# Low parts of the expert weights made on VectorE, and the last quarter of w_in converted one stage later

## The chip, the cores and the metric

One core of a Trainium2 chip runs the whole program once. The time is device microseconds of that core, one launch, median of the runs shown. Besides TensorE (PE, with its weight loads PEld) the core has VectorE (DVE), ScalarE (ACT), GpSimd (POOL) and SyncE (SP), each working through its own instruction queue in order. SP's queue issues nearly all DMAs.

## The reference

Three parts follow one another: an attention over 4 x 8 heads of 576 rows, a routed layer in which each of the 2304 rows goes to one of 8 experts, and a dense layer over all rows. The change touches the weights of the second and third parts:

```
for e in range(E):                                    # x: 2304 x 512
    h = np.maximum(x[mask] @ w1[e], 0.0)              # w1[e]: 512 x 1024
    out[mask] = gate_w[mask, None] * (h @ w2[e])      # w2[e]: 1024 x 512
h = x @ w_in                                          # w_in: 512 x 2048, given as float64
g = np.maximum(h, 0.0) + alpha * np.minimum(h, 0.0)
return (g @ w_out).astype(np.float32)                 # w_out: 2048 x 512, given as float64
```

## The kernel before

**Stages.** Attention and routing come first, with five small tiles of the busiest expert's rows computed beside them. Then come the **expert slots**: seven slots (`NSU`) of 256 rows of one expert each, run by `slot(s)` in `moe`. Then the **dense layer** in `moe2`: five blocks of rows, four of 512 and one of 256.

**Precision.** The slots and the dense layer multiply in a 32-bit matmul format that keeps only part of a float32. So every operand is split into a high part (a cast by ScalarE, L541) and a low part (operand minus high part, L542, on an engine that the caller names), and each product is three matmuls: high by high, low by high, high by low. `split` does this.

**One slot.** The raw weights of the slot's expert lie in the tile `wraw`. `split1` makes `w1h` and `w1l` for one of 8 column tiles f, low part on VectorE, in a ring of 3. `split2` makes `w2h` and `w2l` for one of 8 pieces, numbered c = 0 to 3 and u = 0, 1 (`w2l_21` is c = 2, u = 1), in a ring of 5; in the kernel before c = 0, 1 have their low parts made on GpSimd and c = 2, 3 on VectorE (L637). For each f, 12 matmuls (L700) give `h`, ScalarE takes the high part `hh` and VectorE the low part `hl` (L703). Then 24 matmuls (L720) for each c give `y`, which VectorE or ScalarE copies out (L722, L723). A slot has 192 matmuls. The rows of a later slot are loaded into `L` (`L<-xs`, L566), scaled by GpSimd (L573), transposed by VectorE (`T`, L575) and split into `xh` and `xl`; this is asked for one or two slots ahead.

**Input weights of the dense layer.** While the slots run, `W2in(i)` converts w_in, piece by piece (128 x 256, 32 pieces). A piece comes as 64-bit words by an SP load of 256 KB into one of three buffers (`raw64`), two pieces ahead. `from64` makes a float32 of it with three bit operations on VectorE (L549, L550, L551, tile `xwi`), and then splits it into `wih` and `wil`. Low parts go to GpSimd. Two pieces are done ahead of the slots (`AT0`), then six in each slot, so slots 0 to 4 do the 30 that are left.

**Dense layer.** In a block, for each of 16 column tiles f, 12 matmuls (L776) give `oh`, VectorE applies the activation (`m`, L778, L779) and makes `gl`, ScalarE makes `gh`. Four column tiles later the second product `oy` (L767) uses them. In block 0, `W2out(f)` converts row tile f of w_out in two pieces by the same `from64` and the same three buffers, low parts on GpSimd.

**Order.** The order within each engine's queue is not the source's: a scheduler places instructions by priorities and its own estimate of when each can start. After that each queue is fixed and runs in order; an instruction that waits holds back all behind it on its engine.

Of the kernel before, what the change touches and what calls it, by code (L numbers as in the profile page):

```python
# [538 lines left out]
def split(nc, hi, lo, x, lo_engine):  # L539

    nc.scalar.copy(hi,x)  # L541
    return lo_engine.tensor_tensor(out=lo,in0=x,in1=hi.bitcast(F32),op=ALU.subtract)  # L542
# [68 lines left out]
def moe(tc, stack, router, wts, rows, ep, fp, W2in):  # L611
# [22 lines left out]
        return hi,lo  # L634
    def split2(s,c,u):
        hi=kp.tile([128,4,128],F32R,tag="h2",name=f"w2h{s}_{c}{u}",bufs=5); lo=kp.tile([128,4,128],F32R,tag="l2",name=f"w2l{s}_{c}{u}",bufs=5)
        split(nc,hi,lo,wts.r2[:,4*u:4*u+4,128*c:128*c+128],nc.vector if c>1 else nc.gpsimd)  # L637
        return hi,lo
    W1={}; W2={}; after=[None]
    def whole(s, e):  # L640
# [37 lines left out]
    def slot(s):  # L678
        last=s+1==NSU
        if s==0: load_x(1); after[0]=rows.loaded  # L680
        if not last:
            e=router.reg(0,s+1,[ENG.SP],E-1); ch=router.reg(3,s+1,[ENG.SP],1)
        xh,xl=xin.pop(s)
        H=[]
        def one(s,f):
            if f<8 and (s,f) not in W1: W1[s,f]=split1(s,f)
        def two(i):
            if i<8:
                c,u=divmod(i,2); W2[i]=split2(s,c,u)
                if u and not last: wts.load2(c,e,ch)  # L690
        one(s,0); one(s,1)
        for f in range(8):
            one(s,f+2)
            if f%2 and not last: wts.load1(f//2,e,ch)
            wh,wl=W1.pop((s,f))
            h=hp.tile([128,SL],F32,tag="h",name=f"h{s}_{f}")
            n=0
            for c in range(4):
                for a,b in ((wh,xh),(wh,xl),(wl,xh)):
                    nc.tensor.matmul(h,lhsT=a[:,c],rhs=b[:,c],start=n==0,stop=n==11); n+=1  # L700
            hh=wk.tile([128,SL],F32R,tag=f"hh{f}",name=f"hh{s}_{f}",bufs=1); hl=wk.tile([128,SL],F32R,tag=f"hl{f}",name=f"hl{s}_{f}",bufs=1)
            nc.scalar.activation(out=hh,in_=h,func=AF.Relu)  # L702
            d=nc.vector.scalar_tensor_tensor(out=hl,in0=h,scalar=0.0,in1=hh.bitcast(F32),op0=ALU.max,op1=ALU.subtract)  # L703
            H.append((hh,hl))
            if 2<=f<7: two(f-2)
            if f<6:
                with tc.issue_after(d.ins), tc.issue_after(after[0].ins): W2in(AT0+6*s+f)
            if f==4 and not last: prep_x(s+1)
            if f==5 and s+2<NSU: load_x(s+2)
        o=ep.tile([128,4,SL],F32,tag="eh",name=f"yo{s}",bufs=1)  # L710
        for c in range(4):
            if c and s+1<NSU: one(s+1,c-1)
            y=yp.tile([128,SL],F32,tag="y",name=f"y{s}_{c}")
            n=0
            for u in range(2):
                wh,wl=W2[2*c+u]
                for f in range(4):
                    hh,hl=H[4*u+f]
                    for a,b in ((wh,hh),(wl,hh),(wh,hl)):
                        nc.tensor.matmul(y,lhsT=a[:,f],rhs=b,start=n==0,stop=n==23); n+=1  # L720
                two(2*c+u+5)
            if c%2: nc.vector.tensor_copy(o[:,c],y)  # L722
            else: nc.scalar.copy(o[:,c],y)  # L723
        yr=router.reg(2,s,[ENG.SP],N)
        rows.store(o,yr,SL)
# [18 lines left out]
    ti=wk.tile([128,4],U32,tag="ti",name=f"ti{j}",bufs=1)  # L744
    return load,(hi,lo,ti)

def moe2(tc, stack, wp, fp, ep, win, first, W2out, al, ysT, ytok, out):
    nc=tc.nc
    op=stack.enter_context(tc.tile_pool(name="o_const",bufs=1))
    wk=stack.enter_context(tc.tile_pool(name="o_work",bufs=2))  # L750
# [9 lines left out]
    def block(j):  # L760
# [7 lines left out]
        G=[]; LAG=4 if not last else 1  # L768
        if last: zh=wk.tile([128,16,128],F32R,tag="xh",name="zh",bufs=1); zl=wk.tile([128,16,128],F32R,tag="xl",name="zl",bufs=1)
        for f in range(16):  # L770
            if j==0: W2out(f,woh,wol)
            h=hp.tile([128,512],F32,tag="h",name=f"oh{j}_{f}")
            k=0; fs=slice(128*f,128*f+128)
            for c in range(4):
# [27 lines left out]
def body(tc,q,k,v,mod,wg,bias,w1,w2,w_in,w_out,alpha,out):  # L802
    nc=tc.nc
    with ExitStack() as ctx:
# [37 lines left out]
        def w_out_rows(f,u):  # L842
            r=staged[f,u]=wst.tile([128,256,2],I32,tag="raw64",name=f"wo{f}{u}")
            nc.sync.dma_start(r.rearrange("p d w -> p (d w)"),w_out[128*f:128*f+128,256*u:256*u+256].bitcast(I32))
        def W2out(f,woh,wol):
            for u in range(2):
                if (f,u) not in staged: w_out_rows(f,u)
                c=slice(256*u,256*u+256)
                from64(nc,wst,f"wo{f}{u}",woh[:,f,c],wol[:,f,c],staged.pop((f,u)),nc.gpsimd)
# [1 line left out]
        with nc.allow_non_contiguous_dma("alpha"):  # L851
            nc.sync.dma_start(al,alpha.rearrange("(f p) -> p f",p=128))
        with ExitStack() as s1:
            def W2in_load(i):
                c,p=divmod(i,8); c=3-c
                if c<0: return
                r=staged["in",i]=wst.tile([128,256,2],I32,tag="raw64",name=f"wi{c}{p}")
                return nc.sync.dma_start(r.rearrange("p d w -> p (d w)"),w_in[128*c:128*c+128,256*p:256*p+256].bitcast(I32))
            def W2in(i):
                W2in_load(i+2)  # L860
                c,p=divmod(i,8); c=3-c; ps=slice(256*p,256*p+256)
                if c>=0: from64(nc,wst,f"wi{c}{p}",wir[:,c,ps],wil[:,c,ps],staged.pop(("in",i)),nc.gpsimd)
            W2in_load(0); router.marks[ENG.SP]=W2in_load(1)
            router.marks[ENG.Activation]=running[2]; router.marks[ENG.Pool]=running[1]
            rare=router.flag((ENG.Pool,ENG.Activation,ENG.PE,ENG.DVE,ENG.SP))
# [12 lines left out]
            for u in range(2): w_out_rows(0,u)  # L878
        ee.close()
        with ExitStack() as s2:  # L880
            moe2(tc,s2,wp,fp,ep,(wir,wil),first,W2out,al,ysT,ytok,out)


_INS = ["q", "k", "v", "moe_modality_id", "moe_w_gate", "moe_modality_bias", "moe_w1", "moe_w2", "moe2_w_in", "moe2_w_out", "moe2_alpha"]
# [23 lines left out]
```

## Time and profile before

| | |
|---|---|
| runs | 869.8, 878.67, 886.12 us; median 878.67 |
| profiled execution | 876.93 us, of which the span is 875.2 |
| PE busy | 817.5 us (93%) |
| DVE busy | 529.2 us (60%) |
| ACT busy | 359.9 us (41%) |
| POOL busy | 263.3 us (30%) |
| first matmul of slot 0 | 282.4 us |
| last matmul of slot 6 | 469.2 us |
| end of block 0 of the dense layer | 557.15 us |

"Busy" is the time that instructions of an engine occupied. An average over the span hides that the stages have different limits, so the stages are read apart. A start time and a length are given for each instruction; VectorE takes up the next one a little before the write of the last is acknowledged, so that lengths of neighbours overlap, and the distance from start to start is what one costs in a full queue.

### The profile page before, as it was taken

How to read it: one execution, taken by the hardware profiler on the slowest of the kernel's cores; microseconds unless marked ns; L12 is line 12 of the kernel's file. 1: busy time of each engine (PE TensorE's matmuls, PEld its weight loads, DVE VectorE, ACT ScalarE, POOL GpSimd, SP SyncE). 2: the span in 40 equal slices, each digit the busy share in tenths (PEclk: the TensorE clock that was granted, in tenths of full speed). 3: DMA queues.
4: the chain of work that ended last, by engine and by line, in shares of the span. 5: the costliest groups of instructions: out<-in, count | busy, mean ns of one | idle time of the engine just before them, and what ended most of it. 6: DMA issues, size and time to landing. Idle time of an engine off the chain costs nothing.

```text
span 875.2 us, 16800 instructions
## 1 busy us (share of the span) xinstructions
PE 817.5 (93%) x6175; PEld 698.9 (80%) x6175; DVE 529.2 (60%) x1304; ACT 359.9 (41%) x863; POOL 263.3 (30%) x450
## 2 busy tenths in 40 slices
PE   5797898999997897989999999999999999999997
PEld 3465687778897887989998888888888888888895
DVE  6856756656443997999946998443344333533361
ACT  7697795885423554646542333211121111111120
POOL 9425555366331554535421432100010001000100
PEclk9877889899998998999999999999999999999999
DMA  7735676322332434539501442200020001000100
GB/s 190 172 97 161 187 200 145 101 57 55 78 91 61 98 92 79 135 114 237 157 26 61 132 147 83 85 1 0 1 91 1 0 1 55 13 0 1 37 13 25
DMA packets 96609, 71.74 MB, mean 82 GB/s; under 512 B 40456, under 2 KB 83976, under 8 KB 96520
## 3 DMA queue, kind: packets, MB, share of 16 engines
q1 hardware_dynamic: 93544, 61.02, 26.6%
q0 software_dynamic: 2976, 9.59, 3.2%
q8 instruction: 50, 0.82, 0.4%
q14 instruction: 39, 0.32, 0.1%
HBM read 76.43 MB, written 18.90 MB: 109 GB/s over the span
## 4 chain that ended last, share of the span: by engine, by line
PE 56%; DVE 3%; DMA 2%; issue 2%; ACT 0%; SPq 0%; POOL 0%; POOLq 0%; DVEq 0%; ACTq 0%
PE oh L776 23%; PE oy L767 22%; PE h L700 6%; PE y L720 5%; DMA L<-xs 1%; DVE w1l L542 1%; DVE xwi L551 1%; DVE xwi L550 0%; DMA ytok<-L 0%; DVE hl L703 0%; DVE xwi L549 0%; DMA out<-o,ti 0%; DVE T L575 0%; POOL L L573 0%; DVE xl L542 0%
## 5 line engine op out<-in xcount | busy, mean ns | idle before, releaser
L541 ACT CAST gh<-m 128x512 fp32r<-128x512 f32 (+1 forms) x80 | 44.5, 556 | 241.3 <-DVE m L779 241.3
L776 PE MATMUL oh<-oxh,wil 128*128 128x512 f32 (+1 forms) x320 | 118.9, 372 | 0.0
L776 PE MATMUL oh<-oxh,wih 128*128 128x512 f32 (+1 forms) x320 | 118.9, 371 | 0.0
L776 PE MATMUL oh<-oxl,wih 128*128 128x512 f32 (+1 forms) x320 | 118.6, 371 | 0.0
L778 DVE TENSOR_SCALAR m<-oh,al 128x512 f32<-128x512 f32 (+1 forms) x80 | 55.5, 694 | 91.4 <-PE oh L776 91.4
L793 POOL DMA_INDIRECT out<-o,ti x18 | 17.6, 980 | 308.3 <-ACT o L792 270.6
L767 PE MATMUL oy<-woh,gh 128*128 128x512 f32 x272 | 107.1, 394 | 0.0
L767 PE MATMUL oy<-wol,gh 128*128 128x512 f32 x272 | 106.7, 392 | 0.0
L767 PE MATMUL oy<-woh,gl 128*128 128x512 f32 x272 | 106.5, 393 | 0.0
L700 PE MATMUL h<-xh,w1h 128*128 128x256 f32 x224 | 67.2, 300 | 11.4 <-DVE hl L703 6.3
L542 DVE TENSOR_TENSOR gl<-m,gh 128x512 fp32r<-128x512 f32 (+1 forms) x80 | 48.9, 612 | 40.0 <-ACT gh L541 40.0
L776 PEld LDWEIGHTS oh<-oxh,wil 128*128 128x128 f32 x320 | 60.2, 188 | 11.8
L776 PEld LDWEIGHTS oh<-oxh,wih 128*128 128x128 f32 x320 | 60.1, 188 | 11.5
L776 PEld LDWEIGHTS oh<-oxl,wih 128*128 128x128 f32 x320 | 60.1, 188 | 11.3
L720 PE MATMUL y<-hh,w2h 128*128 128x256 f32 x224 | 61.9, 287 | 4.7 <-ACT hh L702 2.9
L700 PE MATMUL h<-xl,w1h 128*128 128x256 f32 x224 | 65.9, 294 | 0.0
L700 PE MATMUL h<-xh,w1l 128*128 128x256 f32 x224 | 65.6, 293 | 0.0
L720 PE MATMUL y<-hh,w2l 128*128 128x256 f32 x224 | 60.7, 286 | 2.5 <-POOL w2l L542 1.5
L767 PEld LDWEIGHTS oy<-woh,gl 128*128 128x128 f32 x272 | 51.1, 188 | 12.1
L767 PEld LDWEIGHTS oy<-wol,gh 128*128 128x128 f32 x272 | 51.0, 188 | 11.4
L767 PEld LDWEIGHTS oy<-woh,gh 128*128 128x128 f32 x272 | 51.1, 188 | 11.0
L720 PE MATMUL y<-hl,w2h 128*128 128x256 f32 x224 | 59.6, 285 | 0.1
(303 smaller groups left out, 1873.2 us busy)
## 6 DMA issues: line engine op xcount, KB each, us to landing
wraw<-in_moe_w SPq DMA_DIRECT2D x56, 512.0 KB
wi<-in_moe_w_in SPq DMA_DIRECT2D x32, 256.0 KB
wo<-in_moe_w_out SPq DMA_DIRECT2D x32, 256.0 KB
vw<-in_v SPq DMA_DIRECT2D x88, 64.0 KB
xs<-z SPq DMA_DIRECT2D x8, 528.0 KB
ldq<-in_q SPq DMA_DIRECT2D x16, 256.0 KB
ldk<-in_k SPq DMA_DIRECT2D x16, 256.0 KB
ldv<-in_v SPq DMA_DIRECT2D x8, 512.0 KB
```

What stands on the lines that cost most here:

```text
L541: nc.scalar.copy(hi,x)
L542: return lo_engine.tensor_tensor(out=lo,in0=x,in1=hi.bitcast(F32),op=ALU.subtract)
L551: nc.vector.scalar_tensor_tensor(out=xi,in0=hw,scalar=-(1<<30),in1=xi,op0=ALU.bitwise_and,op1=ALU.bitwise_or)
L700: nc.tensor.matmul(h,lhsT=a[:,c],rhs=b[:,c],start=n==0,stop=n==11); n+=1
L720: nc.tensor.matmul(y,lhsT=a[:,f],rhs=b,start=n==0,stop=n==23); n+=1
L767: nc.tensor.matmul(y[t],lhsT=a[:,ts],rhs=b[:,f],start=f==0 and k==0,stop=f==15 and k==2)
L776: nc.tensor.matmul(h[:,:n],lhsT=a[:,c,fs],rhs=b[:,c,:n],start=k==0,stop=k==11); k+=1
L778: nc.vector.tensor_scalar(out=m[:,:n],in0=h[:,:n],scalar1=0.0,scalar2=al[:,f:f+1],op0=ALU.min,op1=ALU.mult)
L793: nc.gpsimd.indirect_dma_start(out=out[:],out_offset=bass.IndirectOffsetOnAxis(ap=ti[:,t:t+1],axis=0),in_=o[:],in_offset=None,bounds_check ...
```

## The change

Low parts of `w2` are made on VectorE for all c. Of w_in, the pieces are put in another order: first columns 0 to 1535 of all four row tiles (24 pieces), then the last quarter, columns 1536 to 2047 (8 pieces). Slots 0 to 4 do four pieces each and slot 5 does two, with the low parts on VectorE as well. The last 8 pieces are converted in block 0 of the dense layer, one in each of column tiles 0 to 7, loaded through the same three buffers, one piece ahead. Low parts of w_out stay on GpSimd.

```diff
     def split2(s,c,u):
...
-        split(nc,hi,lo,wts.r2[:,4*u:4*u+4,128*c:128*c+128],nc.vector if c>1 else nc.gpsimd)
+        split(nc,hi,lo,wts.r2[:,4*u:4*u+4,128*c:128*c+128],nc.vector)
...
-            if f<6:
-                with tc.issue_after(d.ins), tc.issue_after(after[0].ins): W2in(AT0+6*s+f)
+            if f<4 and 4*s+f<22:
+                with tc.issue_after(d.ins), tc.issue_after(after[0].ins): W2in(AT0+4*s+f)
...
-            if j==0: W2out(f,woh,wol)
+            if j==0:
+                W2out(f,woh,wol)
+                if f<8: W2in(f)
...
+        PIECES=[(c,p) for c in (3,2,1,0) for p in range(6)]+[(c,p) for p in range(6,8) for c in range(4)]
+        def W2in_load(i):
+            if i>=len(PIECES): return
+            c,p=PIECES[i]
+            r=staged["in",i]=wst.tile([128,256,2],I32,tag="raw64",name=f"wi{c}{p}")
+            return nc.sync.dma_start(r.rearrange("p d w -> p (d w)"),w_in[128*c:128*c+128,256*p:256*p+256].bitcast(I32))
+        def W2in(i, ahead=2):
+            for j in range(i+1,i+ahead+1):
+                if ("in",j) not in staged and j not in done: W2in_load(j)
+            c,p=PIECES[i]; ps=slice(256*p,256*p+256); done.add(i)
+            from64(nc,wst,f"wi{c}{p}",wir[:,c,ps],wil[:,c,ps],staged.pop(("in",i)),nc.vector)
+        done=set()
...
-            def W2in(i):
-                W2in_load(i+2)
-                c,p=divmod(i,8); c=3-c; ps=slice(256*p,256*p+256)
-                if c>=0: from64(nc,wst,f"wi{c}{p}",wir[:,c,ps],wil[:,c,ps],staged.pop(("in",i)),nc.gpsimd)
...
-            moe2(tc,s2,wp,fp,ep,(wir,wil),first,W2out,al,ysT,ytok,out)
+            moe2(tc,s2,wp,fp,ep,(wir,wil),first,W2out,lambda f: W2in(24+f,1),al,ysT,ytok,out)
```

**VectorE, start of slot 0.** Before:

```order
L542 TENSOR_TENSOR w1l_0_10059<-wraw,w1h_0_10058 128x512
L542 TENSOR_TENSOR w1l_1_10063<-wraw,w1h_1_10062 128x512
L542 TENSOR_TENSOR w1l_2_10067<-wraw,w1h_2_10066 128x512
L542 TENSOR_TENSOR w2l_20_10305<-wraw,w2h_20_10304 128x512
L542 TENSOR_TENSOR w1l_3_10096<-wraw,w1h_3_10095 128x512
L703 SCALAR_TENSOR_TENSOR hl_0_10084<-h_0_10070,hh_0_10083 128x256
L549 TENSOR_SCALAR xwi_10089<-wi_4469 128x256
L550 SCALAR_TENSOR_TENSOR xwi_10089<-wi_4469,xwi_10089 128x256
L542 TENSOR_TENSOR w1l_4_10126<-wraw,w1h_4_10125 128x512
```

The same place with the change:

```order
L542 TENSOR_TENSOR w1l_2_10067<-wraw,w1h_2_10066 128x512
L542 TENSOR_TENSOR w2l_00_10147<-wraw,w2h_00_10146 128x512
L542 TENSOR_TENSOR w2l_01_10181<-wraw,w2h_01_10180 128x512
L542 TENSOR_TENSOR w2l_10_10215<-wraw,w2h_10_10214 128x512
L542 TENSOR_TENSOR w2l_11_10248<-wraw,w2h_11_10247 128x512
L542 TENSOR_TENSOR w2l_20_10289<-wraw,w2h_20_10288 128x512
L542 TENSOR_TENSOR w1l_3_10096<-wraw,w1h_3_10095 128x512
L703 SCALAR_TENSOR_TENSOR hl_0_10084<-h_0_10070,hh_0_10083 128x256
L549 TENSOR_SCALAR xwi_10089<-wi_4469 128x256
L542 TENSOR_TENSOR w1l_4_10126<-wraw,w1h_4_10125 128x512
```

Four low parts of w2 that stood in GpSimd's queue now stand on VectorE ahead of `w1l_3` and `hl_0`. GpSimd's queue holds only the scaling of `L`, once a slot, and one small cast until the slots are over.

**SP's queue, ahead of the load of slot 3's rows.** Before (`xs<-z` clears rows under a condition; then the row load `L_10675`):

```order
L561 DMA xs<-z 1024x1x132
L536 DMA wraw<-in_moe_w 128x8x128
L858 DMA wi_10514<-in_moe_w_in 128x512
L858 DMA wi_10547<-in_moe_w_in 128x512
L858 DMA wi_10582<-in_moe_w_in 128x512
L566 DMA L_10675<-xs 32x8x132
```

With the change (the row load is `L_10643`):

```order
L561 DMA xs<-z 1024x1x132
L536 DMA wraw<-in_moe_w 128x8x128
L854 DMA wi_10498<-in_moe_w_in 128x512
L854 DMA wi_10531<-in_moe_w_in 128x512
L566 DMA L_10643<-xs 32x8x132
```

Two loads of w_in instead of three stand ahead of the row load. The last one ahead waits for a buffer that VectorE frees: before by the operation right behind `hl_4` of slot 1, now by the one right behind `hl_3` of slot 1.

**VectorE, column tile 6 of block 0.** Before:

```order
L778 TENSOR_SCALAR m_6_12983<-oh_6_12970,al 128x512
L551 SCALAR_TENSOR_TENSOR xwo_12956<-wo_12954,xwo_12956 128x256
L779 SCALAR_TENSOR_TENSOR m_6_12983<-oh_6_12970,m_6_12983 128x512
L549 TENSOR_SCALAR xwo_12964<-wo_12962 128x256
L550 SCALAR_TENSOR_TENSOR xwo_12964<-wo_12962,xwo_12964 128x256
L549 TENSOR_SCALAR xwo_13004<-wo_13002 128x256
L551 SCALAR_TENSOR_TENSOR xwo_12964<-wo_12962,xwo_12964 128x256
L542 TENSOR_TENSOR gl_6_12987<-m_6_12983,gh_6_12986 128x512
```

With the change (`xwi_12802` is a piece of w_in; the lines of `moe2` have moved by two):

```order
L780 TENSOR_SCALAR m_6_12977<-oh_6_12964,al 128x512
L542 TENSOR_TENSOR wil<-xwi_12802,wih 128x256
L549 TENSOR_SCALAR xwo_12830<-wo_12828 128x256
L781 SCALAR_TENSOR_TENSOR m_6_12977<-oh_6_12964,m_6_12977 128x512
L550 SCALAR_TENSOR_TENSOR xwo_12830<-wo_12828,xwo_12830 128x256
L549 TENSOR_SCALAR xwo_12838<-wo_12836 128x256
L551 SCALAR_TENSOR_TENSOR xwo_12830<-wo_12828,xwo_12830 128x256
L550 SCALAR_TENSOR_TENSOR xwo_12838<-wo_12836,xwo_12838 128x256
L542 TENSOR_TENSOR gl_6_12981<-m_6_12977,gh_6_12980 128x512
L551 SCALAR_TENSOR_TENSOR xwo_12838<-wo_12836,xwo_12838 128x256
L549 TENSOR_SCALAR xwi_12846<-wi_12800 128x256
```

From one `m` to the next VectorE now converts two pieces of w_out and one of w_in. The pieces of w_out converted beside column tile 6 are those of row tile 4, which the second product needs after column tile 8; before, they were those of row tiles 6 and 7.

## Rows read from the trace of the kernel before

**Rows 1.** Windows: length; busy us of PE, PEld, DVE, ACT, POOL; PEclk; DMA; GB/s.

```profile
282.40:425.20 142.80, 129.05 (x1000) 125.66 (x1000) 129.19 (x221) 80.78 (x179) 74.23 (x59) 0.95 0.52 130
425.20:469.20 44.00, 44.00 (x350) 43.81 (x351) 23.51 (x45) 20.52 (x45) 8.15 (x7) 0.96 0.15 47
469.20:557.15 87.95, 87.95 (x382) 71.46 (x381) 74.89 (x148) 27.32 (x56) 28.01 (x35) 1.00 0.37 114
557.15:646.20 89.05, 89.05 (x385) 72.12 (x385) 37.39 (x54) 13.48 (x22) 4.08 (x6) 1.00 0.08 24
```

**Rows 2.** Page, costliest groups: count | busy us, mean ns | idle before, releaser.

```profile
L700 PE MATMUL h<-xh,w1h 128*128 128x256 f32 x224 | 67.2, 300 | 11.4 <-DVE hl L703 6.3
```

**Rows 3.** Chain that ended last, in order of time: start, us, what.

```profile
328.97 7.81 DMA L<-xs
...
347.13 2.93 PE h L700 x12
...
351.87 2.88 PE h L700 x24
...
487.64 2.79 PE oy L767 x12
```

**Rows 4.** Waits of PE, 277 to 475 us: total us, times, longest.

```profile
PE h L700 <- DVE hl L703: 6.3, 5, 2.3
PE h L700 <- ACT w1h L541: 5.0, 1, 5.0
```

**Rows 5.** Groups of DVE by line, 282 to 469.5 us, columns as in Rows 2.

```profile
L542 DVE TENSOR_TENSOR w1l<-wraw,w1h 128x512 fp32r<-128x512 f32 x56 | 44.5, 800 | 19.4 <-ACT w1h L541 19.3
L542 DVE TENSOR_TENSOR w2l<-wraw,w2h 128x512 fp32r<-128x512 f32 x28 | 24.4, 880 | 4.6 <-ACT w2h L541 2.7 <-POOL w2l L542 1.8
...
L550 DVE SCALAR_TENSOR_TENSOR xwi<-wi,xwi 128x256 int32<-128x256 int32 x30 | 18.4, 615 | 0.2
L551 DVE SCALAR_TENSOR_TENSOR xwi<-wi,xwi 128x256 int32<-128x256 int32 x30 | 17.1, 571 | 0.1
L549 DVE TENSOR_SCALAR xwi<-wi 128x256 int32<-128x256 int32 x30 | 14.8, 497 | 0.9 <-POOL wil L542 0.9
```

**Rows 6.** Instructions by tile, whole span: ns minimum/median/maximum, first and last start.

```profile
L542 DVE TENSOR_TENSOR w1l<-wraw,w1h x56: 644/680/2069, 282.4 to 454.4; 128x512 fp32r<-128x512 f32 x56
L542 DVE TENSOR_TENSOR w2l<-wraw,w2h x28: 677/686/2407, 286.1 to 464.0; 128x512 fp32r<-128x512 f32 x28
L549 DVE TENSOR_SCALAR xwi<-wi x32: 275/282/1673, 270.0 to 416.9; 128x256 int32<-128x256 int32 x32
L550 DVE SCALAR_TENSOR_TENSOR xwi<-wi,xwi x32: 407/413/2023, 270.5 to 417.4; 128x256 int32<-128x256 int32 x32
L551 DVE SCALAR_TENSOR_TENSOR xwi<-wi,xwi x32: 406/414/1517, 271.1 to 421.5; 128x256 int32<-128x256 int32 x32
```

**Rows 7.** Groups of POOL by line, 282 to 469.5 us, columns as in Rows 2.

```profile
L542 POOL TENSOR_TENSOR w2l<-wraw,w2h 128x512 fp32r<-128x512 f32 x28 | 41.9, 1519 | 25.9 <-ACT w2h L541 24.0 <-issue 1.9
L542 POOL TENSOR_TENSOR wil<-xwi,wih 128x256 fp32r<-128x256 f32 x30 | 28.2, 947 | 50.2 <-ACT wih L541 47.1 <-PE y L720 3.1
L573 POOL TENSOR_TENSOR L<-L 128x1024 f32<-128x1024 f32 x6 | 12.5, 2083 | 14.8 <-DMA L<-xs 11.8 <-PE y L720 3.1
```

**Rows 8.** Timeline of DVE: start, us, instruction.

```profile
290.28 2.02 DVE L550 SCALAR_TENSOR_TENSOR xwi<-wi,xwi 128x256 int32<-128x256 int32 x1
...
293.16 0.28 DVE L549 TENSOR_SCALAR xwi<-wi 128x256 int32<-128x256 int32 x1
293.36 0.41 DVE L551 SCALAR_TENSOR_TENSOR xwi<-wi,xwi 128x256 int32<-128x256 int32 x1
293.70 0.68 DVE L542 TENSOR_TENSOR w1l<-wraw,w1h 128x512 fp32r<-128x512 f32 x1
294.30 0.41 DVE L703 SCALAR_TENSOR_TENSOR hl<-h,hh 128x256 fp32r<-128x256 f32 x1
```

**Rows 9.** Timeline of POOL: start, us, instruction.

```profile
290.06 1.96 POOL L573 TENSOR_TENSOR L<-L 128x1024 f32<-128x1024 f32 x1
```

More of the change, by code (lines that the diff above doesn't have):

```diff
@@ L745, in rows2, with moe2 @@
     return load,(hi,lo,ti)
-def moe2(tc, stack, wp, fp, ep, win, first, W2out, al, ysT, ytok, out):
+def moe2(tc, stack, wp, fp, ep, win, first, W2out, W2in, al, ysT, ytok, out):
     nc=tc.nc
@@ L853, in body @@
         with ExitStack() as s1:
[L854 to L858, printed above, removed]
-            def W2in(i):
-                W2in_load(i+2)
-                c,p=divmod(i,8); c=3-c; ps=slice(256*p,256*p+256)
-                if c>=0: from64(nc,wst,f"wi{c}{p}",wir[:,c,ps],wil[:,c,ps],staged.pop(("in",i)),nc.gpsimd)
             W2in_load(0); router.marks[ENG.SP]=W2in_load(1)
```

## The prediction

> **What bounds the kernel now.** I read the windows first. The slots last from 282.4 to 469.2 us, 186.8 us, and block 0 of the dense layer from there to 557.15 [rows 1]. In block 0 PE is busy in every microsecond, and the block is no longer than the next one, in which nothing is converted (87.95 against 89.05): what other engines do there is hidden today. In slots 0 to 4 PE is busy 129.1 of 142.8 us while DVE is busy 129.2; in slots 5 and 6 PE is full and DVE only about half. So a stall to be won lies in slots 0 to 4.
>
> How much is there: six groups of 224 matmuls, one of them in [rows 2], are 1344. The chain of waits shows 24 of them in 2.88 us when PE runs free, 0.120 each [rows 3]; 1344 of them are 161.3 us. The slots lose 186.8 - 161.3 = **25.5 us**. It is not all waiting: after a stall PE comes back at the lower of its two clocks, and 12 matmuls take 2.93 us in place of 1.44 [rows 3]. One such loss, 1.5 us, comes at the start, behind the 5.0 us wait for the first weight part, which nothing here changes [rows 4]. That leaves **24.0 us**. The largest named wait is that of a first-layer matmul for `hl` on DVE, 6.3 us in five pieces [rows 4].
>
> Why DVE is late is in its own groups. The means are far above the medians: 800 against 680 ns for `w1l`, 880 against 686 for `w2l`, and 615, 571 and 497 against 413, 414 and 282 for the three bit operations [rows 5, 6]. Times their counts, the five are longer than at the median by 6.4, 5.2, 6.0, 4.7 and 6.3 us, together **28.6 us**. POOL is what runs then: L550 took 2.02 us from 290.28 on, and POOL's scaling of `L` ran from 290.06 for 1.96 us [rows 8, 9].
>
> **The change, part by part.** *GpSimd's work in the slots.* Its low parts of w2 and w_in go, 41.9 + 28.2 us of its time; the scaling of `L` stays, six times, 12.5 us [rows 7]. One scaling can lengthen DVE's work by 2.02 - 0.41 = 1.6 us [rows 6, 8], six by 9.6. So of the 28.6 us of lengthening 19.0 go, 66%. I let PE's loss fall in the same proportion: 24.0 x 0.66 = **15.9 us less**. The ends are 0, if the lengthening was hidden behind other waits, and 24.0.
>
> The page "SBUF — State Buffer" of the Trainium skill, section "Who interferes with whom", says that a VectorE instruction with two SBUF inputs and a GpSimd instruction that reads SBUF share a port which one of them holds for its whole length while the other blocks. The trace agrees as far as the pair of rows at 290 us goes (2.02 us beside 1.96), while over the slots DVE was lengthened by 28.6 us beside 82.6 us of GpSimd's work. By that rule of the Trainium skill the share that goes would be that of GpSimd's time, which is the first rival.
>
> *VectorE's work in the slots.* In a full queue a low part of 512 columns costs 0.60 us from start to start (293.70 to 294.30), the first bit operation 0.20, the others 0.34 [rows 8]. 28 more low parts of w2 are 16.8 us; 20 of w_in (four for each of slots 0 to 4) at the price of a bit operation of the same 256 columns, which is the nearest row, 6.8; two more in slot 5 are 0.7; eight pieces fewer at 0.20 + 2 x 0.34 = 0.88 take 7.0 away. Net 17.3 more, against 19.0 less: DVE is no fuller than before. What matters is where it stands. In slot 0 the order puts `w2l_00` to `w2l_11` ahead of `w1l_3` and `hl_0`, 2.4 us that ran beside DVE before. I take 0 for it: between `hl_7` of a slot and matmul h_3 of the next PE has, by its order, some 110 of a slot's 192 matmuls, 13.2 us, and DVE owes there six low parts of w2, one or two of w1, a transpose and a split of rows twice as wide (an estimate of 1.2 us each, from the 0.60) and a few short ones, about 8 us. The cover is 5.2 us; without it, up to 2.4 us a slot, 16.8 in all.
>
> *Eight pieces into block 0.* Each costs DVE 0.88 + 0.34 = 1.22 us, **9.8 us** in all. DVE was busy 74.9 of 87.95 us there [rows 1], so 84.7: it fits, with 3.3 us over. ScalarE takes 8 casts at 27.3 of 87.95. The order shows that DVE now makes row tile 4 of w_out beside column tile 6. PE asks for it four groups after oh_6, 4 x 2.79 = 11.2 us [rows 3]; from `m` to the last bit operation of that row tile stand ten operations, three of them of 512 columns and the others of 256, some 4 us by the prices above. Of the last quarter, column tile 12 is the first to ask, and the piece made last for it stands ahead of column tile 7. So I take **0**, with 0 and 9.8 as ends.
>
> *Transfers.* Eight loads of 256 KB move on SP's queue from the slots to block 0, 2.1 MB on 88 us, 24 GB/s on top of 114, where slots 0 to 4 move 130 [rows 1]. They stand between loads of w_out in the same three buffers, so three loads a column tile, 5.58 us of PE, take turns. I count 0. In the slots the load of slot 3's rows now stands behind two loads of w_in instead of three, and is let go one column tile of work earlier. That load took 7.81 us to land [rows 3]; this helps, and I book nothing for it.
>
> **Sum.** The profiled execution took 876.93 us. 876.93 - 15.9 = 861.0. The median of the runs is 1.7 us above the profiled one: 862.8. I forecast **862 us**.
>
> **Rivals.** *Almost all of the loss goes.* For it: in proportion to GpSimd's time, not to lengthening, 70.1 of 82.6 us go, 85%, 20.4 us, so 858; with all 24.0, 855. This is also what the section "Who interferes with whom" of the Trainium skill's "SBUF — State Buffer" would make of it. Against: the scaling of `L` stays at the very point where rows of the next slots enter. Chance 0.20.
>
> *Late rows take the stall's place.* A transpose of rows stands in DVE's queue right behind `hl_7`, with all later low parts behind it. From `hl_3`, behind which the load of a later slot's rows is let go, to `hl_7` pass four column tiles, with the second-layer matmuls between them some 65 matmuls, 7.8 us; landing and scaling take 7.81 + 2.08 = 9.9 us [rows 3, 7]. So DVE stands 2.1 us, more where SP's queue holds the load up. If that and the 1.6 us of a scaling use up the cover of 5.2, the 2.4 us of low parts are lost in each of five slots, and 12 us come back: 874.8. For it: the slots get shorter and the transfers don't. Against: rows are asked for one slot or two ahead. Chance 0.17.
>
> *Block 0 becomes VectorE's.* If 3.3 us over is not enough, because w_out's low parts stay on GpSimd and still lengthen DVE's bit operations, 9.8 us come back: 872.6. Chance 0.12.
>
> *Slower.* If the lengthening is not GpSimd's doing, then DVE, busy 129.2 of 142.8 us, gets 17.3 us more in the slots and 9.8 in block 0, nothing less, and PE waits for all of it: 878.7 + 27.1 = 906. It decides if the mean of `w1l` stays near 800 ns with GpSimd quiet. Against it stands the pair of rows at 290 us. Chance 0.06.
>
> The page "Perfetto Trace Analysis" of the Trainium skill, section "Optimizing Scalar/DVE Operations", speaks for this rival: when VectorE is saturated, it says, handing some work to ScalarE or even GpSimd may make sense (it adds that the port they share may undo the gain), and this change takes work back. The trace bears out that VectorE is nearly full, 129.2 of 142.8 us.
>
> That the change does not do what it says can be left out: in GpSimd's queue only the scaling and one cast are left in the slots.
>
> **How the numbers follow.** The forecast's own case, 858 to 868, has 0.45. The range takes in the first rival and all of the second and third with some scatter of the runs: 852 to 878. A measurement of this kernel can tell about 2% from no change, that is 861.1 and 896.2. Faster than that: the first rival and nearly half of the forecast's case, 0.40. Slower: 0.05. Within: 0.55.
>
> **What would show it.** Right: from first to last slot matmul about 171 us; mean of `w1l` near 700 ns; no wait of PE for a GpSimd low part; block 0 still about 88 us with DVE above 83. Wrong: PE waits in block 0 for a low part of w_out or `gl`; or DVE idle before `T` with matmul h_3 or h_4 waiting behind it; or means of DVE's groups that don't fall.

## The result and the profile after

| | before | with the change |
|---|---|---|
| median of 20 runs, us | 878.59 (869.8 to 886.12) | 869.04 (865.7 to 876.25) |
| ratio | | 0.9917, interval 0.9896 to 0.9939 |
| profiled execution, us | 876.93, span 875.2 | 865.7, span 864.0 |
| DVE busy, us | 529.2 | 535.7 |
| POOL busy, us | 263.3 | 194.8 |
| first matmul of slot 0, us | 282.40 | 281.48 |
| first slot matmul to first matmul of block 1, us | 274.6 | 264.3 |
| first matmul of block 0 to first of block 1, us | 91.73 | 97.40 |

The change makes the kernel 0.8% faster; 1.9% was forecast. The last two lines say where the rest went. The last matmuls of slot 6 stand between the first ones of block 0, so its length is taken here from its first matmul to the first of block 1. That is 91.73 us when PE never stops, as before; with the change it is 5.7 us longer. Of these PE stands idle for 3.5 (97.40 - 93.87), and its matmuls take 2.1 longer (93.87 against 91.73).

Windows of the kernel after, columns as in [rows 1]: slots 0 to 4, slots 5 and 6, block 0, block 1, and block 0 from its first matmul.

```profile
281.48:408.50 127.02, 122.74 (x996) 121.52 (x996) 117.68 (x233) 78.59 (x170) 13.83 (x7) 0.98 0.58 128
408.50:452.20 43.70, 43.10 (x354) 42.68 (x354) 27.65 (x59) 20.78 (x47) 0.00 (x0) 1.00 0.14 49
452.20:545.80 93.60, 90.07 (x383) 70.79 (x382) 85.20 (x177) 27.91 (x60) 28.36 (x33) 1.00 0.38 123
545.80:634.80 89.00, 89.00 (x386) 72.19 (x385) 39.20 (x57) 15.79 (x26) 5.55 (x6) 1.00 0.10 32
...
448.37:545.77 97.40, 93.87 (x410) 74.41 (x409) 85.20 (x177) 28.45 (x62) 28.36 (x33) 1.00 0.37 118
```

Against [rows 1], slots 0 to 4 are shorter by 15.8 us, and POOL fell there from 74.2 to 13.8 us busy. In block 0 PE is no longer busy all the time (90.07 of 93.60), and DVE is busy for 85.20.

Waits of PE after, first from 265 to 452.5 us, then from 440 us to the end (total us, times, longest).

```profile
PE h L700 <- ACT w1h L541: 5.1, 1, 5.1
PE y L720 <- DVE yo L722: 2.5, 1, 2.5
PE h L700 <- DVE hl L703: 2.0, 4, 0.7
PE y L720 <- ACT hh L702: 0.3, 1, 0.3
...
PE oy L767 <- ACT woh L541: 2.9, 3, 1.6
PE oy L767 <- POOL wol L542: 0.5, 1, 0.5
```

The wait for `hl`, 6.3 us in [rows 4], is down to 2.0. New are the last two: the second product of block 0 waits for parts of w_out. Before, PE waited for nothing after the slots.

The same L700 group of the page as in [rows 2], where the wait for `hl` stood first, and the group of `oy` that has the new wait.

```profile
L767 PE MATMUL oy<-woh,gh 128*128 128x512 f32 x272 | 106.6, 396 | 2.9 <-ACT woh L541 2.9
...
L700 PE MATMUL h<-xh,w1h 128*128 128x256 f32 x224 | 64.9, 290 | 7.1 <-ACT w1h L541 5.1
```

### The profile page after: what moved, and what is told of

It is laid out like the page before. It is cut to its first block, busy times and chain, and to the rows that moved or that the text cites. A ratio compares the mean times of both kernels' runs of the same rounds, so it can differ in the third digit from the quotient of the medians.

```text
span 864.0 us, 16760 instructions
## 1 busy us (share of the span) xinstructions
PE 805.8 (93%) x6175; PEld 688.1 (80%) x6175; DVE 535.7 (62%) x1364; ACT 360.7 (42%) x863; POOL 194.8 (23%) x390
## 4 chain that ended last, share of the span: by engine, by line
PE 50%; DVE 8%; DMA 4%; issue 4%; ACT 0%; POOL 0%; SPq 0%; POOLq 0%; DVEq 0%; ACTq 0%
PE oh L778 18%; PE oy L767 18%; PE h L700 7%; PE y L720 7%; DMA wo<-in_moe_w_out 2%; DVE xwo L551 1%; DMA oT<-ysT 1%; DVE xwo L550 1%; DVE w1l L542 1%; DVE xwo L549 1%; DMA wi<-in_moe_w_in 1%; DVE m L780 1%; DVE xwi L551 1%; DVE w2l L542 0%; DVE hl L703 0%
## 5 line engine op out<-in xcount | busy, mean ns | idle before, releaser
L700 PE MATMUL h<-xh,w1h 128*128 128x256 f32 x224 | 64.9, 290 | 7.1 <-ACT w1h L541 5.1
L778 PEld LDWEIGHTS oh<-oxh,wih 128*128 128x128 f32 x320 | 60.2, 188 | 11.5
L778 PEld LDWEIGHTS oh<-oxl,wih 128*128 128x128 f32 x320 | 60.2, 188 | 11.2
L700 PE MATMUL h<-xl,w1h 128*128 128x256 f32 x224 | 64.2, 287 | 0.0
L700 PE MATMUL h<-xh,w1l 128*128 128x256 f32 x224 | 63.9, 286 | 0.0
```

What stands on the lines that cost most here:

```text
L778: nc.tensor.matmul(h[:,:n],lhsT=a[:,c,fs],rhs=b[:,c,:n],start=k==0,stop=k==11); k+=1
```

## The experiments

Two questions: what won the slots, and what stalls block 0? For the slots the theory is that GpSimd's working lengthens VectorE's operations; the rival is that moving the eight pieces out, or no longer waiting for GpSimd's results, did it. For block 0, theory A is that VectorE has too much to do there, theory B that three loads a column tile turn around too slowly in three buffers.

In the table T runs from the first slot matmul to the first matmul of block 1, B is what block 0 lasts beyond PE's own time for it (91.73 us in most orders), and T - B is what the slots make of it. L is the time from the first matmul of block 0 at which the last low part of w_out begins; in TensorE's order of the kernel before, and without waits, PE asks for that row tile of w_out at 89.0 us. All are of one profiled execution each; the two pairs of equal kernels show how far such numbers go apart (T - B 258.6 and 258.2, 259.0 and 262.0; B 5.7 and 8.3).

| kernel | median us | ratio to before | interval | T | B | T - B | L |
|---|---|---|---|---|---|---|---|
| before | | 1 | | 274.6 | 0 | 274.6 | 72.9 |
| the change | 869.0 | 0.9917 | 0.9896 to 0.9939 | 264.3 | 5.7 | 258.6 | 94.1 |
| the change, again | 872.0 | 0.9915 | 0.9878 to 0.9952 | 266.5 | 8.3 | 258.2 | 96.6 |
| all pieces in slots 0 to 4 | 871.3 | 0.9968 | 0.9929 to 1.0006 | 266.8 | 0 | 266.8 | 72.3 |
| the move alone | 882.8 | 1.0071 | 1.0037 to 1.0105 | 285.0 | 13.4 | 271.6 | 99.2 |
| GpSimd work for nobody | 896.0 | 1.0206 | 1.0161 to 1.0251 | 290.5 | 8.6 | 281.9 | 96.9 |
| buffers of their own | 867.1 | 0.9919 | 0.9886 to 0.9953 | 263.8 | 4.1 | 259.7 | 91.6 |
| no loads | 865.8 | 0.9882 | 0.9822 to 0.9942 | 262.2 | 3.6 | 258.6 | 91.8 |
| no conversion | 865.2 | 0.9858 | 0.9806 to 0.9910 | 261.3 | 0 | 261.3 | 77.1 |
| spread over slots 0 to 6 | 863.3 | 0.9859 | 0.9812 to 0.9906 | 259.0 | 0 | 259.0 | 75.4 |
| spread, again | 866.8 | 0.9857 | 0.9811 to 0.9903 | 262.0 | 0 | 262.0 | 75.5 |
| spread, fewer in slot 4 | 865.0 | 0.9829 | 0.9784 to 0.9874 | 257.9 | 0 | 257.9 | 75.0 |
| low parts of w_out on VectorE | 864.7 | 0.9821 | 0.9780 to 0.9863 | 259.5 | 0 | 259.5 | 99.4 |
| the same, fewer in slot 4 | 858.3 | 0.9812 | 0.9771 to 0.9853 | 255.7 | 0 | 255.7 | 85.5 |

For the two kernels with the low parts of w_out on VectorE, T is taken to the end of block 1, less its 89.05 us, since the orders of the two blocks overlap. Medians come from different chips; ratios are to the kernel before on the same one. In TensorE's order of the kernel before, PE does not wait where the last part begins by 77.1 us, and waits where it begins at 91.6 or later; of the two kernels with another order, the last two, more is said below.

**The two halves of the change.** First the move undone:

```diff
-            if f<4 and 4*s+f<22:
-                ... W2in(AT0+4*s+f)
+            if f<6 and 6*s+f<30:
+                ... W2in(AT0+6*s+f)
...
-                if f<8: W2in(f)
```

> Against the changed kernel, only the move is undone: all 30 pieces of w_in that are left are converted in slots 0 to 4, six a slot, low parts of w2 and w_in on VectorE. Theory (GpSimd's absence wins the 16 us of the slots, the eight pieces cost block 0 its 5.6 us): block 0 is back at 88 us; eight more pieces are 8 x 1.22 = 9.8 us more for VectorE in slots 0 to 4, where it is busy 117.7 of 127.0 us now, so part of it shows there: slots 172 to 180 us, time 865 to 873. Rival (the slots were won by moving the pieces out, not by GpSimd's absence): slots back near 186 us, time 878 or more.

Block 0 is back at 91.72 us; the slots (T - B) win 7.8 us over before in place of 16.0. The time, 871.3, lies within what was expected, and its interval does not exclude no change.

Then the move alone, low parts left on GpSimd:

```diff
-        split(...,nc.vector)
+        split(...,nc.vector if c>1 else nc.gpsimd)
...
-            from64(...,staged.pop(("in",i)),nc.vector)
+            from64(...,staged.pop(("in",i)),nc.gpsimd)
```

> Against the kernel before, only the move is made: eight pieces of w_in go to block 0, low parts of w2 (c = 0, 1) and w_in stay on GpSimd. Theory (GpSimd's work is what lengthens VectorE's): GpSimd still has some 75 of its 82.6 us in the slots, so the slots win at most 2 to 4 us (183 to 185) and block 0 loses about as much again, 3 to 6 us: time 877 to 882. Rival (the move frees VectorE in the slots): slots about 177 us, time near 873.

The slots win 3.0 us, as the theory has it, but block 0 loses 13.4 us, over twice the upper end. The rival is out. Windows of block 0 from its first matmul: the move alone, then (in the second fence) all pieces in the slots.

```profile
459.66:564.81 105.15, 98.19 (x411) 76.36 (x409) 87.32 (x171) 29.27 (x64) 33.04 (x42) 0.97 0.35 111
```

```profile
457.37:549.09 91.72, 91.72 (x410) 75.05 (x409) 74.74 (x148) 27.83 (x58) 27.99 (x34) 1.00 0.36 110
```

VectorE has six instructions fewer with the move alone than with the change (171 against 177), since eight low parts are GpSimd's, and is busy longer: 87.32 against 85.20. So its work in block 0 is not of a fixed length; it grows with what GpSimd does. That was not expected, and it led to the last experiments below.

**GpSimd alone.** 28 GpSimd operations are added to the changed kernel; nobody reads what they write. `spare` is a stretch of `wil` whose columns are filled only in block 0, so the rows call it `wil`.

```diff
         split(nc,hi,lo,wts.r2[:,4*u:4*u+4,128*c:128*c+128],nc.vector)
+        if c<2: nc.gpsimd.tensor_tensor(out=spare,in0=hi.bitcast(F32),in1=hi.bitcast(F32),op=ALU.subtract)
```

> The changed kernel with 28 GpSimd operations added to the slots, of the shape of w2's low parts, paced by the casts of w2 as those were; nobody reads what they write. Theory (GpSimd working lengthens VectorE's operations): 41.9 of the 82.6 us that GpSimd had are back, VectorE's operations are lengthened by some 14 us again, mean of w2l near 900 ns, slots 178 to 182 us, time 876 to 880. Rival (what held PE was the wait for GpSimd's results or the order on VectorE): slots 171 to 172, time 869.

The slots lose 23.3 us, over twice as much as expected, and the time, 896.0 us, lies above the 876 to 880 named; the rival is out. Groups of DVE in the slots, columns as in [rows 2]; first the changed kernel.

```profile
L542 DVE TENSOR_TENSOR w2l<-wraw,w2h 128x512 fp32r<-128x512 f32 x56 | 43.3, 793 | 4.3 <-ACT w2h L541 4.2
L542 DVE TENSOR_TENSOR w1l<-wraw,w1h 128x512 fp32r<-128x512 f32 x56 | 38.0, 687 | 15.8 <-ACT w1h L541 15.8
L703 DVE SCALAR_TENSOR_TENSOR hl<-h,hh 128x256 fp32r<-128x256 f32 x56 | 23.4, 419 | 2.3 <-ACT hh L702 2.3
...
L542 DVE TENSOR_TENSOR wil<-xwi,wih 128x256 fp32r<-128x256 f32 x22 | 9.0, 418 | 0.0
...
L575 DVE STREAM_TRANSPOSE T<-L 128x1024 f32<-128x1024 f32 x6 | 7.4, 1235 | 3.4 <-POOL L L573 3.4
L542 DVE TENSOR_TENSOR xl<-T,xh 128x1024 fp32r<-128x1024 f32 x6 | 7.3, 1217 | 0.2 <-ACT xh L541 0.2
```

The same with the added GpSimd work, and that work itself, whose group is POOL's.

```profile
L542 DVE TENSOR_TENSOR w2l<-wraw,w2h 128x512 fp32r<-128x512 f32 x56 | 54.8, 999 | 3.0 <-ACT w2h L541 3.0
L542 DVE TENSOR_TENSOR w1l<-wraw,w1h 128x512 fp32r<-128x512 f32 x56 | 42.5, 768 | 22.6 <-ACT w1h L541 22.2
L704 DVE SCALAR_TENSOR_TENSOR hl<-h,hh 128x256 fp32r<-128x256 f32 x56 | 23.2, 414 | 2.2 <-ACT hh L703 2.2
L542 DVE TENSOR_TENSOR wil<-xwi,wih 128x256 fp32r<-128x256 f32 x22 | 11.2, 517 | 0.0
...
L542 DVE TENSOR_TENSOR xl<-T,xh 128x1024 fp32r<-128x1024 f32 x6 | 8.1, 1358 | 0.0
L575 DVE STREAM_TRANSPOSE T<-L 128x1024 f32<-128x1024 f32 x6 | 7.4, 1237 | 3.6 <-POOL L L573 3.6
```

```profile
L638 POOL TENSOR_TENSOR wil<-w2h 128x512 fp32r<-128x512 f32 x28 | 36.7, 1311 | 54.4 <-ACT w2h L541 52.9
```

Four groups of VectorE got longer, by 11.5, 4.5, 2.2 and 0.8 us, beside 36.7 us of GpSimd work: about half a microsecond for each of GpSimd's. Two did not change, `hl` (419, 414 ns) and `T` (1235, 1237). The four subtract one SBUF tile from another; `hl` has one input in PSUM, and `T` has one input. The section "Who interferes with whom" of the Trainium skill's "SBUF — State Buffer" draws the line just there: a VectorE instruction with two SBUF inputs contends with a GpSimd one that reads SBUF, and one with at most one SBUF input does not, unless it runs in a mode that uses two ports. The trace agrees for these six groups. L549 has one input and was lengthened in block 0, as the last experiments show; the section counts its kind (`tensor_scalar`) among those that can enter such a mode, and no run here shows whether it did. The bit operations hardly tell anything in the slots: of 66 only three met a GpSimd operation there.

Single instructions say the same more sharply. With the added work 26 low parts of w1 and w2 took over 0.75 us; each of them began while a GpSimd operation ran and ended 0.55 us after the end of one. Of the 76 beside which no GpSimd operation ran, none took more than 0.69 us.

PE's waits in the slots of this kernel are for VectorE and not for GpSimd.

```profile
PE h L701 <- DVE hl L704: 11.7, 6, 3.2
...
PE y L721 <- DVE w2l L542: 4.9, 4, 1.8
```

VectorE waits for GpSimd as in the changed kernel, for scaled rows: 6.5 us against 6.3. The order on VectorE and TensorE is the same but for a few places, most of them in the first slot. So the lengthening costs the slots more than the change had won. Of the 23.3 us PE stands idle for 11.8, and its matmuls take 11.5 longer at a granted clock of 0.93 in the slots, against 0.99. Block 0 loses 8.6 us in this kernel, hardly more than the changed kernel itself (5.7 and 8.3).

**Block 0: work or loads?** Three kernels, each a change of the changed one. Six of the eight pieces get two buffers that lie idle in block 0:

```diff
-            r=staged["in",i]=wst.tile([128,256,2],I32,tag="raw64",...)
+            if i<26: r=wst.tile([128,256,2],I32,tag="raw64",...)
+            elif i%2: r=ep.tile([128,8,SE],F32,tag="eh",...)...
+            else: r=ep.tile([128,4,SE],F32,tag="eo",...)...
+            staged["in",i]=r
```

> The changed kernel, where six of the eight pieces of w_in in block 0 are loaded into two buffers of their own, so that w_out has its three to itself. Theory A (VectorE has too much to do in column tiles 0 to 8 of block 0): VectorE's idle time for loads of w_out, 2.5 us, may go, but PE still waits: block 0 at 92 us or more, time 867 to 869. Theory B (three loads a column tile turn around too slowly in three buffers): block 0 at 88 to 89 us, time 863 to 865.

Six loads are left out, the operations stay:

```diff
             c,p=PIECES[i]
+            if i>25: staged["in",i]=wir[:,c,0:512].bitcast(I32)...; return
```

> The changed kernel without the loads of the last six pieces of w_in: their bit operations read words of the w_in tile that is there already (so the last quarter of the columns holds wrong values), with the same shapes and strides. All of VectorE's work in block 0 stays; w_out has the three buffers to itself. Theory A (too much work on VectorE): block 0 stays at 92 us or more, time 867 to 869. Theory B (loads and buffers): block 0 at 88 to 89 us, time 863 to 865.

The conversions are left out, the loads stay:

```diff
+        nc.gpsimd.memset(wir[:,:,1536:]...); nc.gpsimd.memset(wil[:,:,1536:]...)
...
+            if i>23:
+                r=staged.pop(("in",i)); nc.vector.tensor_copy(wil[:,c,256*p:256*p+2],r[:,0:2,1]); return
             from64(...)
```

> The changed kernel with all eight loads in block 0 kept, but each piece read by one tiny copy on VectorE in place of its conversion (the last quarter of w_in's columns is zero, filled by GpSimd before the slots). Theory A (too much work on VectorE): about 9 us of it are gone, block 0 at 88 us, time 863 to 865. Theory B (loads and buffers): PE waits as before, block 0 at 92 us or more, time 867 to 869.

B is 4.1, 3.6 and 0 us. Without loads PE still stalls; without conversions it doesn't, though all eight loads take their turns. Theory A holds and B falls as the main cause. The times alone would not have settled it: 867.1 and 865.2 us are about where A has them, and 865.8 lies between the two theories. Whether the loads add anything stays open: 3.6 and 4.1 are 1.6 to 4.7 us less than 5.7 and 8.3, two executions of one kernel that differ by 2.6. Nor do the two edits change loads alone: VectorE waits 3.6 us there for GpSimd to give back a buffer of `xwo`, 0.5 us in the changed kernel. And without the conversions a load's buffer comes free sooner.

**The pieces elsewhere.** Slots 5 and 6 had VectorE busy 27.65 of 43.70 us.

```diff
-            if f<4 and 4*s+f<22:
-                ... W2in(AT0+4*s+f)
+            if f<4+(s>4):
+                ... W2in(AT0+4*s+f+(s>5))
...
-                if f<8: W2in(f)
```

> The changed kernel with the last eight pieces in slots 5 and 6, where VectorE is busy 27.7 of 43.7 us, in place of block 0 (four pieces in slots 0 to 4 as in the change, five in slots 5 and 6). If block 0's 5.6 us come from the pieces standing there, by whatever mechanism: block 0 at 88 us, slots unchanged at 171, time 863 to 864. Rival (VectorE in slots 5 and 6 has no room where the pieces stand, or their loads hold up the queue): slots 174 to 176, time 867 to 869.

B is 0, as the theory had it, and T - B is 259.0 against 258.6. The median, 863.3, is as expected too, but the kernel before took 874.8 us on that chip, so the ratio tells more: 0.9859, against 0.9917 of the change. Beside the changed kernel on one chip:

> The changed kernel itself, for a comparison on one chip: 869, block 0 at 97 us from its first matmul, slots at 171.

> The kernel with all pieces in the slots, 4, 4, 4, 4, 4, 5 and 5 of them, beside the changed one on one chip: 5 to 6 us less than the changed kernel, block 0 at 92 us from its first matmul.

872.0 and 866.8 us, 5.2 less. T - B is 262.0 against 258.2 in this pair: the slots gave back 3.8 of 8.3 us, so the rival is not quite out. Against the first execution of the spread kernel the slots are 3.0 us longer, at a granted clock of 0.96 in place of 0.98. The repeated execution of the changed kernel also has the larger stall in block 0, 8.3 us. Its PE waits there, 4.8 us, are for the same two tiles:

```profile
PE oy L767 <- ACT woh L541: 3.4, 4, 1.7
...
PE oy L767 <- POOL wol L542: 1.4, 4, 0.5
```

One wait was left in slot 4 of the spread kernel: PE for `yo`, 2.2 and 2.6 us, behind a transpose of rows that waits for GpSimd's scaling.

```diff
+            if f<(4,4,4,4,2,6,6)[s]:
+                ... W2in(AT0+(0,4,8,12,16,18,24)[s]+f)
```

> All pieces of w_in in the slots, 4, 4, 4, 4, 2, 6 and 6 of them. In slot 4 a load of w_in takes 5.5 us, the scaling and transposing of rows stand behind it, and PE waits 2.2 us for yo. Theory (two pieces fewer in slot 4 let the rows in sooner): that wait goes, 1 to 3 us less than with 4, 4, 4, 4, 4, 5, 5: time 861 to 863. Rival (VectorE, at 27.7 us with two pieces, comes to 40 of 43.7 us in slots 5 and 6 and is late there, or the load is slow for another reason): 863 to 866.

The wait for `yo` is gone. That for `hl` rose from 1.8 to 3.4 us, 1.6 of it in one piece early in slot 5, which now has six pieces. T is 257.9 against 259.0 and 262.0; the ratios, 0.9829 and 0.9857, overlap. Both theories are partly right, and the sum is not told apart from nothing.

**GpSimd in block 0.** The move alone had shown that VectorE's time there grows with GpSimd's. So the low parts of w_out go to VectorE too, which gets 32 more operations in the stage where it is the limit:

```diff
-                from64(nc,wst,f"wo{f}{u}",woh[:,f,c],wol[:,f,c],staged.pop((f,u)),nc.gpsimd)
+                from64(nc,wst,f"wo{f}{u}",woh[:,f,c],wol[:,f,c],staged.pop((f,u)),nc.vector)
```

> The changed kernel with the low parts of w_out made on VectorE too, so that GpSimd is nearly silent in block 0. Theory (GpSimd's 28 us of low parts lengthen VectorE's operations there): 32 low parts at 0.34 are 10.9 us more for VectorE, while its bit operations fall from 586, 508 and 323 ns to about 415, 415 and 285, some 11 us less; VectorE's sum stays at 84 to 86 us, and block 0, 97.4 us now from its first matmul, comes to 94 to 97 us: time 865 to 869. Rival (VectorE has simply too many operations, GpSimd or not): 10.9 us come on top, block 0 at 105 us or more, time 876 or more.

The rival would have had 876 or more. It is 864.7, just under the theory's 865, and PE does not wait in block 0 at all, where the theory left it 94 to 97 us. Windows of blocks 0 and 1 together, from the first matmul of block 0: first the changed kernel, then this one.

```profile
448.37:634.79 186.42, 182.89 (x794) 146.62 (x793) 124.40 (x234) 44.24 (x88) 33.91 (x39) 1.00 0.24 77
```

```profile
453.63:634.41 180.78, 180.78 (x794) 147.09 (x793) 121.81 (x266) 43.27 (x88) 5.34 (x7) 1.00 0.26 79
```

VectorE has 32 instructions more and is busy 2.6 us less. Its groups in block 0 say why; first the changed kernel with POOL's low parts, then this one.

```profile
L551 DVE SCALAR_TENSOR_TENSOR xwo<-wo,xwo 128x256 int32<-128x256 int32 x30 | 17.6, 586 | 0.2
L550 DVE SCALAR_TENSOR_TENSOR xwo<-wo,xwo 128x256 int32<-128x256 int32 x30 | 15.2, 508 | 0.2
...
L549 DVE TENSOR_SCALAR xwo<-wo 128x256 int32<-128x256 int32 x30 | 9.7, 323 | 2.9 <-DMA wo<-in_moe_w_out 2.5
...
L542 POOL TENSOR_TENSOR wol<-xwo,woh 128x256 fp32r<-128x256 f32 x32 | 28.2, 882 | 111.2 <-ACT woh L541 61.5 <-PE y L720 49.7
```

```profile
L542 DVE TENSOR_TENSOR wol<-xwo,woh 128x256 fp32r<-128x256 f32 x29 | 12.1, 419 | 0.1
L551 DVE SCALAR_TENSOR_TENSOR xwo<-wo,xwo 128x256 int32<-128x256 int32 x28 | 11.7, 419 | 0.1
L550 DVE SCALAR_TENSOR_TENSOR xwo<-wo,xwo 128x256 int32<-128x256 int32 x28 | 11.7, 419 | 0.1
L549 DVE TENSOR_SCALAR xwo<-wo 128x256 int32<-128x256 int32 x28 | 8.1, 291 | 6.3 <-DMA wo<-in_moe_w_out 6.1
```

586, 508 and 323 ns became 419, 419 and 291: over 30 pieces of w_out that is (167 + 89 + 32) x 30 = 8.6 us. One pair of rows of the changed kernel shows a single case: POOL's low part runs from 482.42 to 483.44, and VectorE's two-input operation begun at 482.76 ends 0.28 us after it.

```profile
482.42 1.02 POOL L542 TENSOR_TENSOR wol<-xwo,woh 128x256 fp32r<-128x256 f32 x1 [4.16 <-ACT woh L541]
```

```profile
482.76 0.96 DVE L551 SCALAR_TENSOR_TENSOR xwo<-wo,xwo 128x256 int32<-128x256 int32 x1
```

So GpSimd's low parts do lengthen VectorE's work in block 0. That this lengthening is what stalled PE is not shown. The last low parts of w_out come no sooner than in the changed kernel: they now stand in VectorE's own queue, which waits 6.1 us for loads of w_out (2.5 in the changed kernel). The rows give the first and the last start of these low parts, in the kernel before, the changed one and this one; from the first matmul of block 0 the last starts are 72.9, 94.1 and 99.4 us (L in the table).

```profile
L542 POOL TENSOR_TENSOR wol<-xwo,woh x32: 735/748/1215, 469.4 to 538.1; 128x256 fp32r<-128x256 f32 x32
```

```profile
L542 POOL TENSOR_TENSOR wol<-xwo,woh x32: 731/745/1690, 452.5 to 542.4; 128x256 fp32r<-128x256 f32 x32
```

```profile
L542 DVE TENSOR_TENSOR wol<-xwo,woh x32: 415/418/426, 458.0 to 553.0; 128x256 fp32r<-128x256 f32 x32
```

PE does not wait because its own order is another. The scheduler has put matmuls of block 1's first product among those of block 0, and PE asks for the last row tile of w_out at 101.2 us, not at 89.0. The next rows count the matmuls of the first product (the first number with x): 192 in the changed kernel from the first matmul of block 0 to the first of block 1, and 226 here in 91.73 us.

```profile
448.37:545.77 97.40, 46.47 (x192) 36.09 (x193) 22.77 (x32) 0.00 (x0) 1.00 0.37 118
```

```profile
453.63:545.36 91.73, 55.33 (x226) 42.27 (x226) 25.76 (x36) 0.00 (x0) 1.00 0.37 115
```

Three things differ at once, then: the lengthening, the wait for GpSimd to give back the two buffers of `xwo` (0.5 us in the changed kernel), and TensorE's order. No run has GpSimd silent in block 0 with eight pieces and the old order, so which of them saved the 5.7 to 8.3 us stays open; that w_out came later, not sooner, speaks for the order.

Last, both findings together, with four pieces left in block 0:

```diff
+            if f<(4,4,4,4,2,4,4)[s]:
+                ... W2in(AT0+(0,4,8,12,16,18,22)[s]+f)
...
+                if f<4: W2in(f)
...
-            moe2(...,lambda f: W2in(24+f,1),...)
+            moe2(...,lambda f: W2in(28+f,1),...)
```

> Low parts of w_out on VectorE as in the run before, and of w_in 4, 4, 4, 4, 2, 4, 4 pieces in the slots and the last four in block 0. Theory: block 0 loses nothing, as with all eight pieces (91.73 us from its first matmul), and the wait for yo in slot 4, 2.4 us, goes as it did with two pieces there: about 2 us less than with eight pieces in block 0, ratio to the kernel before 0.979 to 0.981. Rival (slots 5 and 6, with four pieces in place of two and none, give the 2 us back in waits for hl): ratio 0.982 to 0.983.

B is 0, no wait for `yo` is left, `hl` costs 2.1 us, and T is 255.7, 3.8 us under the run before. TensorE's order is nearly the old one here: PE asks for the last row tile at 90.1 us, and its last low part begins at 85.5, in time, with half as many pieces. The ratio, 0.9812, lies between what the two theories said and is not told apart from 0.9821. This is the lowest time of all, and both kernels with GpSimd silent in block 0 beat the changed one: ratios of 0.9812 and 0.9821 against 0.9915, and on one chip 864.7 against 872.0 us.

## Why the prediction was right in the slots and wrong in block 0

*The slots, 15.9 us less: right, the size in part by luck.* T - B fell by 16.0 us, and from the first to the last slot matmul it is 170.9 us, where 171 was named. The mean of `w1l` is 687 ns, and PE waits there for no low part of GpSimd. Windows of the slots, before and with the change:

```profile
282.40:469.23 186.83, 173.08 (x1349) 169.50 (x1350) 152.70 (x265) 101.29 (x223) 82.38 (x65) 0.95 0.43 110
```

```profile
281.48:452.34 170.86, 165.98 (x1349) 164.34 (x1350) 145.33 (x291) 99.36 (x215) 13.83 (x7) 0.99 0.47 108
```

Of the 16.0 us, 8.9 are time in which PE stood idle, and 7.1 are its matmuls' own, at a granted clock of 0.95 and of 0.99. That the lengthening is GpSimd's doing is shown by the work for nobody, and the rival "slower" is out: the change took work back from GpSimd, and VectorE's groups got shorter. The Trainium skill's "Perfetto Trace Analysis", section "Optimizing Scalar/DVE Operations", which spoke for this rival (hand work from a saturated VectorE even to GpSimd), adds itself that the port they share may undo the gain. The trace bears out this second half: 36.7 us of work given to GpSimd cost the slots 23.3.

The rule by which the 15.9 was reckoned, that PE's loss falls in the proportion of the lengthening, does not hold by itself. With all pieces in the slots GpSimd is as silent, and they win 7.8 us; the move alone won 3.0; only both together made 16.0. (The five differences times their counts are 29.4 us, not 28.6, which changes the proportion by a hundredth.)

*VectorE's added work in the slots, 0: borne out in the sum.* The one late place was slot 4, 2.5 us: there the rival of late rows came true on a small scale. But the room was used up: with eight pieces more in slots 0 to 4 they lose 8.2 us again (266.8 against 258.6).

*Eight pieces into block 0, 0: this is the step that failed.* In place of 0 it cost 5.7 us, and 8.3 in the other execution. VectorE's busy time was forecast at 84.7 us and is 85.2, but "it fits, with 3.3 us over" does not follow from that sum. What counts is when the parts of w_out are ready, and the time left over did not lie where it was needed. Windows of the kernel before, while w_out was converted and behind it:

```profile
477.00:537.00 60.00, 60.00 (x261) 48.72 (x260) 57.66 (x120) 20.02 (x43) 22.85 (x28) 1.00 0.42 132
537.00:557.00 20.00, 20.00 (x89) 16.20 (x88) 10.04 (x15) 5.82 (x10) 2.13 (x3) 1.00 0.19 53
```

VectorE was busy for 57.7 of 60 us there, and for 10.0 of the 20 behind, where pieces converted in column tiles 0 to 7 could not go. The last low part of w_out began at 72.9 us, 16 us before PE asked for it. With the change it began at 94.1, so 9.8 us of added work delayed it by 21 us. Part of that can be the activations of further column tiles, which PE went on to meanwhile and which stand in the same queue, and waits in order (2.5 us for loads, 2.5 for `oxh`); the parts were not measured apart. The one margin that was worked out, row tile 4 beside column tile 6, held, but with 2.3 us in place of the 7 reckoned (11.2 less some 4); from row tile 8 on PE waited.

That VectorE is late was the third rival, at 0.12 and with 9.8 us to come back; 5.7 and 8.3 did. Its stated cause was GpSimd's low parts of w_out lengthening the bit operations. The lengthening is there: in block 0 of the kernel before, the three bit operations on `xwo` had means of 536, 521 and 371 ns and medians of 416, 415 and 281, which over 30 pieces is 9.5 us among the 74.9. More GpSimd work also made the stall larger (13.4 us for the move alone). That there would be no stall without it is not shown, since the run that took it away has another order on TensorE.

*Transfers, 0: not shown to cost anything in block 0*, as above. In slot 4 the chain that ends in the wait of 2.5 us has a load of w_in in it, 5.9 us.

*The sum.* 861.0 was forecast for the profiled execution and 865.7 measured. The difference of 4.7 is 5.7 in block 0, less 0.1 in the slots and 0.9 by which the slots began earlier (281.48 against 282.40), in a stage that the change does not touch. The median lies 3.3 us above that execution, not 1.7; a larger stall in block 0 in other executions, as in the repeated one, would make that, but only that one was seen.

## What to carry to other kernels

A sum of busy time against the length of a stage does not say that work fits. Ask for each part when it is ready and when it is asked for: here 16 us of margin before, and none with the change, at a busy time that was forecast within 0.5 us. Busy time also holds the lengthening by another engine, so read each group's mean against its median in every stage that the change touches. Where GpSimd subtracts SBUF tiles beside a VectorE that is nearly full, giving VectorE that work as well can cost it nothing in sum: with 32 operations more it was busy 2.6 us less in two blocks. But an edit that moves work between engines can change the order on a third, so compare that order before naming a cause. Work that must wait for a place goes where the windows show the engine half idle, here slots 5 and 6.

## What was not expected of the hardware

- GpSimd work whose results nobody reads made the changed kernel 2.1% slower than the kernel before (interval 1.6 to 2.5), where without it it is 0.8% faster: 36.7 us of it lengthened VectorE's two-input operations by 19.0 us and the slots by 23.3 us. Half of that is the clock: PE's matmuls took 177.5 us in the slots at a granted clock of 0.93, and 166.0 at 0.99 in the changed kernel.
- VectorE's low parts of w1 and w2 were not slowed in proportion but held up: with the added work each of the 26 long ones ended 0.55 us after the end of a GpSimd operation.
- The one-input bit operation L549 was lengthened too: a mean of 371 ns in block 0 before and 323 with the change, 291 with GpSimd silent. Each long one ended 0.15 us after the end of a GpSimd operation.
